# Retention visits with the crossed half of the values issued ahead of the next chunk's scores

## The chip, the cores and the metric

One Trainium2 chip, one core of it. The time is the device time of one execution in microseconds (us). Kernels that are compared ran in turns on the same chip. "TensorE" is the matrix engine (PE in the profile, PEld its weight loads), "VectorE" is DVE, "ScalarE" is ACT.

## The reference, cut to what matters

```python
# retention: 4 batches, 8 heads, 768 steps, head width 64
for t in range(S):
    state = gamma * state + k[t] (outer) v[t]
    y[t]  = scale * q[t] @ state
# then x = y as (3072, 512), and an MLP
h = x @ w_in                                   # 512 -> 2048
g = h * erf(softplus(h))
out = g @ w_out                                # 2048 -> 512
```

The kernel computes retention in 24 chunks of 128 steps. After the first 512 tokens it interleaves one chunk, a "visit", with each half-group of the MLP: visits j = 7 to 23 are the ones that the change touches. All arithmetic is fp32.

## The kernel before: the parts that matter

A visit works on 64-row, 64-column tiles of the array, so that four small matmuls are in it at once. A chunk is two half chunks of 64 steps. The scores inside a half are masked (`AM`) and applied to the values; the "straight" half of these products (`of_values(False)`) goes into the r banks of PSUM, the "crossed" half (`of_values(True)`) must go elsewhere. It goes into `other`, the two hp banks that also take the scores of the next chunk: scores in columns 0 to 63 of each head pair, crossed values in columns 64 to 127.

```python
def sub_scores(j):                                          # L485 is its matmul: 16 of 64x64
    for hp in range(HP):
        for a, s in itertools.product(range(2), range(2)):
            ...
            nc.tensor.matmul(SC[j][s][t, hp, :D], KT[j][own, hp, t], QT[j][own, hp, t], start=True, stop=True)

def sub_mask(j):                                            # L492: two VectorE operations
    AM[j] = ret.tile([P, 2, HP, C], F32, name="am")
    for s in range(2):
        nc.vector.tensor_tensor(AM[j][:, s, :, :D], SC[j][s][:, :, :D], causal_d[...], op=ALU.mult)

def sub_visit(j, g):
    ...
    other = SC[j + 1] = [ret_psum(ps_h) for _ in range(2)]  # the two hp banks

    def of_values(crossed):                                 # L535: 8 of 64x64
        ...
        nc.tensor.matmul(other[a][own, u % 2, D:] if crossed else pp[a][own, u % 2, t],
                         V[j][t, 2 * u + r, :], AM[j][t, r, u, :D], ...)

    if c:
        of_state(0)                                         # L520: 8 of 64x64
    ...                                                     # L556: products that renew the state
    nc.vector.tensor_tensor(state, state, new[0], op=ALU.add)   # L561 (a copy, L563, where c == 0)
    of_values(False)
    if j + 1 < NJ:
        sub_scores(j + 1)
        sub_mask(j + 1)
    of_values(True)
    of_state(1)                                             # L520 again, with the renewed state
    ...                                                     # ScalarE copies and VectorE adds to xT
```

Cuts are marked with dots. Counts of matmuls in the comments and in the text are calls of `nc.tensor.matmul`. The trace shows each of these calls as two MATMULs and two weight loads, so x16 in a line of the profile is 8 calls. After a visit TensorE goes on with the projection of the MLP (L784) on the full array.

## Time and profile before

| | before |
|---|---|
| time, median of 4 runs | 712.20 us (711.41 to 713.44) |
| span of the profiled execution | 711.2 us |
| TensorE busy | 688.0 us, 97% |
| VectorE, ScalarE busy | 54%, 36% |
| one visit, first load of the straight values to first load of the projection | 2.41 us |
| from one visit to the next | 27.9 us |

The busy line says which engine is the bound. The waits say where it stands still, the chain of waits says whether that standing still sets the end, and the timeline of a single visit gives the lengths. A word on the third row: a matmul that has started counts as busy until its modelled end, so a wait that begins while one is in flight is partly booked as busy time. The prediction below shows the lines.

### The profile page before, as it was taken

The numbers are of one execution on the slowest core, as the hardware profiler recorded it, in microseconds if no ns is written. First come the engines' busy times: TensorE is split into PE (matmuls) and PEld (weight loads), VectorE is DVE, ScalarE is ACT, GpSimd is POOL, SyncE is SP. The second block draws the span as 40 slices with busy tenths as digits, with TensorE's granted clock in tenths as the row PEclk, the third lists the DMA queues.
The fourth block names the chain that finished last, engine by engine and source line by source line (L and its number), as shares of the span: only waits on it lengthen the run. The fifth ranks groups of instructions, "written<-read, shape, count | busy, mean of one in ns | idle before, by whom it ended". The sixth has DMA issues, their size and how long they took to land.

```text
span 711.2 us, 14317 instructions
## 1 busy us (share of the span) xinstructions
PE 688.0 (97%) x6214; PEld 583.6 (82%) x6214; DVE 385.3 (54%) x581; ACT 256.9 (36%) x291; POOL 6.6 (1%) x21
## 2 busy tenths in 40 slices
PE   8798999999999999999999999999999999999997
PEld 7544454486998998998988989989989889899996
DVE  4689999264954553553554454544553463253234
ACT  3256462325144144143242341441432423414431
POOL 1000000010000000000000000000000000000000
PEclk9999999999999999999999999999999999999999
DMA  9999863102322221222222222312221210000000
GB/s 189 205 252 240 196 180 75 28 1 42 103 37 39 72 42 34 70 36 44 61 44 42 66 40 42 70 36 42 46 60 31 44 47 1 2 30 1 2 30 30
DMA packets 147215, 47.11 MB, mean 66 GB/s; under 512 B 135760, under 2 KB 136016, under 8 KB 147152
## 3 DMA queue, kind: packets, MB, share of 16 engines
q1 hardware_dynamic: 144640, 45.66, 29.4%
q10 hardware_dynamic: 2512, 0.53, 0.5%
q8 instruction: 48, 0.79, 0.5%
q14 instruction: 15, 0.12, 0.1%
HBM read 39.86 MB, written 6.29 MB: 65 GB/s over the span
## 4 chain that ended last, share of the span: by engine, by line
PE 90%; DVE 4%; DMA 3%; SPq 1%; issue 1%; ACT 0%; DVEq 0%
PE hp L712 35%; PE o L784 34%; PE o L655 8%; PE hp L642 4%; PE hp L535 2%; DMA w_in_sb<-in_moe_w_in_dram 2%; PE r L520 1%; PE hp L485 1%; DVE am L492 1%; PE o L556 1%; DMA w_out_sb<-in_moe_w_out_dram 1%; SPq L114 1%; DVE w_out_sb L211 1%; DMA kq<-in_q_dram 1%; PE r L535 1%
## 5 line engine op out<-in xcount | busy, mean ns | idle before, releaser
L712 PE MATMUL hp<-xs,w_in_sb 128*128 128x128 f32 x1280 | 149.8, 275 | 0.0
L712 PEld LDWEIGHTS hp<-xs,w_in_sb 128*128 128x128 f32 x1280 | 147.8, 192 | 1.6 <-issue 0.5
L784 PE MATMUL o<-w_out_sb,h 128*128 128x256 f32 x640 | 141.7, 379 | 0.0
L784 PEld LDWEIGHTS o<-w_out_sb,h 128*128 128x128 f32 x640 | 121.6, 190 | 16.5
L712 PE MATMUL hp<-xT,w_in_sb 128*128 128x128 f32 x960 | 113.7, 275 | 0.0
L712 PEld LDWEIGHTS hp<-xT,w_in_sb 128*128 128x128 f32 x960 | 111.9, 192 | 1.9 <-issue 1.0
L784 PE MATMUL o<-w_out_sb,e 128*128 128x256 f32 x480 | 112.1, 383 | 0.0
L631 DVE TENSOR_TENSOR e<-h,e 128x1024 f32<-128x1024 f32 x42 | 49.5, 1221 | 102.7 <-ACT e L612 102.7
L784 PEld LDWEIGHTS o<-w_out_sb,e 128*128 128x128 f32 x480 | 88.2, 190 | 11.6
L642 PE MATMUL hp<-xT,w_in_sb 128*128 128x512 f32 x128 | 56.5, 595 | 1.3 <-ACT h L645 0.9
L737 DVE TENSOR_TENSOR h<-h,hp 128x512 f32<-128x512 f32 x20 | 13.7, 686 | 75.3 <-PE hp L712 75.3
L607 ACT ACT_TABLE_LOAD x24 | 30.8, 1283 | 60.9 <-issue 45.5
L642 PEld LDWEIGHTS hp<-xT,w_in_sb 128*128 128x128 f32 x128 | 23.9, 190 | 30.2 <-issue 28.2
L612 ACT ACTIVATE e<-e 128x2048 f32<-128x2048 f32 (+1 forms) x23 | 42.2, 1837 | 0.2
L607 ACT ACTIVATE e<-h 128x2048 f32<-128x2048 f32 x22 | 42.0, 1910 | 0.2
L725 DVE TENSOR_TENSOR h<-h,hp 128x512 f32<-128x512 f32 x20 | 13.8, 689 | 51.4 <-PE hp L712 51.4
L574 ACT COPY xT<-r 128x256 f32<-128x256 f32 x32 | 10.4, 375 | 71.9 <-PE r L520 71.9
L735 ACT COPY h<-hp 128x512 f32<-128x512 f32 x20 | 11.7, 586 | 60.2 <-PE hp L712 60.2
L730 ACT COPY h<-hp 128x512 f32<-128x512 f32 x20 | 11.7, 587 | 57.9 <-PE hp L712 57.9
L728 ACT COPY h<-hp 128x512 f32<-128x512 f32 x20 | 11.7, 587 | 55.3 <-PE hp L712 55.3
L612 ACT ACT_TABLE_LOAD x24 | 30.8, 1283 | 0.4
L723 ACT COPY h<-hp 128x512 f32<-128x512 f32 x20 | 11.8, 588 | 48.6 <-PE hp L712 48.6
(123 smaller groups left out, 685.2 us busy)
## 6 DMA issues: line engine op xcount, KB each, us to landing
w_out_sb<-in_moe_w_out_dram SPq DMA_DIRECT2D x14, 512.0 KB, 5.6
kq<-in_k_dram SPq DMA_DIRECT2D x24, 256.0 KB, 3.5
v<-in_v_dram SPq DMA_DIRECT2D x24, 256.0 KB, 3.1
w_in_sb<-in_moe_w_in_dram SPq DMA_DIRECT2D x12, 512.0 KB, 9.1
out_dram<-r SPq DMA_DIRECT2D x23, 256.0 KB, 2.4
kq<-in_q_dram SPq DMA_DIRECT2D x256, 16.0 KB, 1.7
kb<-in_k_dram SPq DMA_DIRECT2D x256, 16.0 KB, 1.7
w_out_sb<-in_moe_w_in_dram SPq DMA_DIRECT2D x4, 512.0 KB, 7.8
```

The source lines that it names most:

```text
L535: nc.tensor.matmul(other[a][own, u % 2, D:] if crossed else pp[a][own, u % 2, t], V[j][t, 2 * u + r, :], AM[j][t, r, u, :D], start=crossed ...
L607: nc.scalar.activation(E[g], HS[g], AF.Softplus)
L612: nc.scalar.activation(E[g][:, half], E[g][:, half], AF.Erf)
L631: nc.vector.tensor_tensor(E[g][:, half], HS[g][:, half], E[g][:, half], op=ALU.mult)
L642: nc.tensor.matmul(p, w_in_of(ft, kk), XC[0][:, kk, :], start=(kk == 0), stop=(kk == n_k - 1))
L655: nc.tensor.matmul(O[0][tt].rearrange("p (d c) -> p d c", d=2), E[g][:, u * TCH + tt * P : u * TCH + (tt + 1) * P], w_out_of(ft), start=(f ...
L712: nc.tensor.matmul(bank[:, u, :], w_in_sb[:, s, IN[a], kk, u * P : (u + 1) * P], XS[m][b][:, kk, :], start=(p in (1, 2, 5) and u == 0 and ...
L723: nc.scalar.copy(h["11"], flat)
L725: nc.vector.tensor_tensor(h["11"], h["11"], flat, op=ALU.add)
L728: nc.scalar.copy(h["12"], flat)
L737: nc.vector.tensor_tensor(h["12"], h["12"], flat, op=ALU.add)
L784: nc.tensor.matmul(O[m][i][:, half, :], G[g][a][:, u * P : (u + 1) * P], w_out_sb[:, s, OUT[b], u, :], start=i not in started, stop=(s == ...
```

## The change

Its intent: take the masks' read of the hp banks out from between two writes of TensorE to these banks.

```diff
         of_values(False)
+        of_values(True)
         if j + 1 < NJ:
             sub_scores(j + 1)
             sub_mask(j + 1)
-        of_values(True)
         of_state(1)
```

## The prediction

> **What bounds the kernel now.** I read the page's busy line first, then the waits of TensorE and of its weight loads, then the chain of work that ended last, and at the end the timeline of single visits of retention.
>
> The page, busy time by engine (us, share of the span, instructions):
>
> ```profile
> PE 688.0 (97%) x6214; PEld 583.6 (82%) x6214; DVE 385.3 (54%) x581; ACT 256.9 (36%) x291; POOL 6.6 (1%) x21
> ```
>
> TensorE is the bound: 97% busy, and in the whole-kernel chain it holds 90% of the span. VectorE and ScalarE have half of their time and more free. So a gap of TensorE is time, and an instruction of another engine is time only where TensorE waits for it.
>
> The waits (who waited for whom: us in total, times, longest):
>
> ```profile
> PE hp L535 <- DVE am L492: 8.5, 16, 0.5
> PEld hp L535 <- DVE am L492: 10.7, 16, 0.7
> ```
>
> These are the longest waits of TensorE and of its weight loads for another engine; all the others of TensorE are from the first part of the kernel. L535 are the matmuls of the values, those that go to the hp banks are the crossed half; L492 is the mask on the next chunk's scores. 16 waits, one for each visit that has a next chunk to score: the visits are j = 7 to 23, and the last has none.
>
> The chain through one visit (start us, us, what; "x16" counts matmuls and weight loads together, so 8 matmuls):
>
> ```profile
> 383.79 0.23 PE r L535 x16
> 384.03 0.54 PE hp L485 x32
> 384.56 0.42 DVE am L492
> 384.98 0.04 issue
> 385.02 0.32 PE hp L535 x2
> 385.35 0.01 issue
> 385.36 0.40 PE hp L535 x11
> 385.75 0.01 PE r L520
> 385.76 0.05 PE hp L535 x3
> 385.81 0.23 PE r L520 x15
> 386.04 0.41 PE o L784
> ```
>
> The mask is on the chain. And it costs more than the wait that the table above counts: the first crossed matmul starts when the first of the two masks is done (385.02), the second waits for the second mask (385.36), and only then do the other six stream. The table's 8.5 us leaves that second wait out, because one matmul is in flight in it.
>
> The timeline of the same visit (start us, us, engine, line; idle before in brackets):
>
> ```profile
> 383.56 0.33 PEld L535 LDWEIGHTS r<-am,v 64*64 64x64 f32 x16
> 383.79 0.56 PEld L485 LDWEIGHTS hp<-qT,kT 64*64 64x64 f32 x32
> 383.85 0.42 DVE L561 TENSOR_TENSOR state<-state,o 128x256 f32<-128x256 f32 x1 [0.18 <-PE r L556]
> ...
> 384.55 0.76 DVE L492 TENSOR_TENSOR am<-hp,causal_d 128x256 f32<-128x256 f32 x2 [0.28 <-PE hp L485]
> 385.02 0.59 PEld L535 LDWEIGHTS hp<-am,v 64*64 64x64 f32 x13 [0.67 <-DVE am L492]
> ...
> 385.97 1.59 PEld L784 LDWEIGHTS o<-w_out_sb,e 128*128 128x128 f32 x8
> ```
>
> From the first weight load of the first half of the values (383.56) to the first one of the projection that follows (385.97) a visit takes 2.41 us. This is the stretch that the change rearranges. I read it from the starts of weight loads, as the ends of matmuls are modelled.
>
> **What the Trainium skill says.** "PSUM — Partial Sum Buffer", section "PSUM bank collisions raise a hardware error": two engines may not touch one bank in the same quadrant of partitions at once, even in different columns, so an access is to be guarded by the bank and not by the address. The trace of before agrees in its effect: the mask reads columns 0 to 63 of each head pair, the crossed values write columns 64 to 127, no datum passes between them, and TensorE waited all 16 times. It is a wait made by sharing, and an order of issue can take it away.
>
> "TensorEngine Tiling (Array Packing)", section "Key Properties": tiles of the array run independently, but a change of the tiling mode drains the array. The trace agrees with the first: sixteen 64x64 matmuls of L556, modelled at 0.22 us each, go from 383.09 to 383.56, 0.47 us, so 29 ns each. For the second see the last visit below. All matmuls that are exchanged are 64x64, so no mode change is added.
>
> "TensorE: Matmul & The Clock Gate", section "Wait — 56ns, not 53.3ns?": however small a matmul, starts are about 25 ns or more apart. The 29 ns above lie a little over that, so I expect no small matmul to go faster than 29 ns after the change.
>
> **The change part by part.** It removes no instruction and adds none; VectorE's, ScalarE's and the DMA queue's orders are the same. On TensorE, in each of the 16 visits, eight crossed values pass ahead of sixteen scores. The order of writing in the two hp banks becomes crossed values, scores, then the masks read; after that nothing of TensorE touches these banks in the visit.
>
> - Removed: the wait of the crossed values for both masks. The compiled order shows what they wait for instead: for the previous reader of the hp banks (ScalarE for the first, VectorE's addition L737 for the second). The scores waited for just that before, at the same place of the stream, so this moves and doesn't grow. In most visits it is satisfied in time (L737 from 382.97 for 0.69 us, so 383.66, against 383.79); in four visits before, the scores' loads show some 0.05 to 0.15 us of it, and they will keep it.
> - Added: the second product with the state, L520, gets a wait of its own for the state's addition L561, which the wait for the masks used to cover. L561 ends at 384.27.
> - New length of the stretch: 8 values 0.235, 8 crossed 0.235, 16 scores 0.47 (all at 29 ns), then the 8 products with the state and the change to the projection's full array. The last visit, which has no scores, shows that tail already:
>
> ```profile
> 634.46 0.13 PEld L535 LDWEIGHTS r<-am,v 64*64 64x64 f32 x1
> ...
> 635.26 0.32 PEld L520 LDWEIGHTS r<-qT,state 64*64 64x64 f32 x16 [0.19 <-DVE state L561]
> ...
> 635.65 1.38 PEld L784 LDWEIGHTS o<-w_out_sb,e 128*128 128x128 f32 x7
> ```
>
> From L520's first load to L784's first is 0.39 us: 0.235 of issue and some 0.155 of drain. The sum is 0.235 + 0.235 + 0.47 + 0.39 = 1.33 us, against 2.41: 1.08 us less in a visit. The chain gives the same in another way: 386.04 - 383.79 = 2.25 us before, and 40 matmuls at 29 ns are 1.17 us after, also 1.08 less. The visits that are longer before (2.47 to 2.54 us) are so by the wait for L737, which stays, so the gain is taken to be equal. 16 x 1.08 = 17.3 us, all of it on TensorE's own path. 712.74 - 17.3 = 695.4; I allow 0.2 us for small bubbles: **695.6 us**, 2.4% less.
>
> **The rivals.**
>
> First, a wait for the state takes the place of the mask's. In the last visit L520 waits 0.19 us for L561 with nothing but the crossed values before it. With sixteen scores between, L520 is due at 383.56 + 0.235 + 0.235 + 0.47 = 384.50, and the state is ready at 384.27 plus the 0.05 us that a release took there (L535 at 385.02 after a mask that ended by 384.97). 0.18 us of slack, and against it that TensorE may need its release some time ahead of the moment of use. If it all went wrong by 0.2 us a visit, 3.2 us are lost: 698.8.
>
> Second, the gain is only what the waits' table says, 16 x 0.53 = 8.5 us on TensorE or 10.7 on its weight loads, because the second half of the wait is hidden anyway. That would give 702 to 704. Against it: at 385.36 the chain itself shows six crossed matmuls and eight products still to come, whose time lies behind both masks.
>
> Third, what TensorE gains it gives back at a later wait, as the gating or the transposes have less time. For this: the gate's exponentials share one buffer. Against it: the elements of a group are gated by VectorE at 370.7, and the projection that needs them comes at 377.5, 7 us later; ScalarE's wait before the copies of retention's result is 4.3 us; the mask itself is needed a whole visit later, 28 us. A visit shorter by 1 us can't use up 7. VectorE's mask will start some 0.23 us later, beside ScalarE's copies from other banks, and TensorE waits for neither. I give this little weight. A lower granted clock, now 0.997, with a busier array has as little for it.
>
> **Range and chances.** The gain in a visit could lie between 0.9 (a bubble at L520 or slower streaming of 40 mixed matmuls) and 1.18 us (the drain shorter): 14.4 to 18.9 us, so 693.8 to 698.3. I take 693.8 to 699.0 as the range, with the longer side at the slow end. The 2% line lies at 698.5, a gain of 0.89 us in a visit. The first rival in full would just miss it, the second and third would miss it clearly: together 0.13. Slower would need a new wait longer than the one removed: 0.01 at most. So faster 0.86, same 0.13, slower 0.01.
>
> **What would show each step.** In the waits of TensorE, the line L535 on L492 must be gone, and no line of 16 waits of more than 0.1 us each take its place; a line L520 on L561 would be the first rival. In a visit's timeline, the stretch from the first load of the first values to the projection's first load must be near 1.33 us and the distance between two visits shrink from 27.9 to 26.8 us. TensorE's busy share should rise to 98 or 99% with the instructions' counts unchanged. If the stretch shrinks by 1.08 us but the distance between visits less, the third rival holds; if the stretch shrinks by about 0.5, the second.

## The result, and the profile after

The changed kernel took 695.06 us in the median of 4 runs (694.28 to 696.97) against 712.20 us before. The ratio is 0.9762, with a 95% interval of 0.9735 to 0.9789. Ratios here are the mean time of one kernel's fast runs over that of the other's of the same rounds, so not quite the ratio of the medians. The results are correct.

The busy line of the page after:

```profile
PE 679.8 (98%) x6214; PEld 579.7 (84%) x6214; DVE 383.8 (55%) x581; ACT 257.2 (37%) x291; POOL 6.6 (1%) x21
```

The instructions are the same in number. The span fell by 711.2 - 694.0 = 17.2 us, and TensorE's busy time fell by 688.0 - 679.8 = 8.2 us of that, although it does the same matmuls: those 8.2 us were waiting that had been booked as busy. The other 9.0 us were booked as idle. So the idle column of before showed only about half of what there was to gain.

The longest waits of TensorE after, and below the dots the one line of its weight loads on the state (us in total, times, longest):

```profile
PE r L461 <- DVE am L433: 2.7, 2, 2.5
PE r L408 <- issue: 1.6, 2, 1.0
...
PEld r L520 <- DVE state L561: 0.2, 1, 0.2
```

The line of 16 waits of L535 on L492 is gone; what leads now is from the first part of the kernel, and it was there before. The single wait on the state is that of the last visit, also there before.

The chain of waits through the same visit as in the prediction, j = 14 (start us, us, what):

```profile
374.99 0.23 PE r L535 x16
375.23 0.23 PE hp L535 x16
375.46 0.47 PE hp L485 x32
375.93 0.23 PE r L520 x16
376.16 0.41 PE o L784
```

No other engine is in it any more: 376.16 - 374.99 = 1.17 us, against 386.04 - 383.79 = 2.25 before.

The timeline of this visit after (start us, us, engine, line; idle before in brackets):

```profile
374.76 0.33 PEld L535 LDWEIGHTS r<-am,v 64*64 64x64 f32 x16
374.99 0.33 PEld L535 LDWEIGHTS hp<-am,v 64*64 64x64 f32 x16
375.23 0.56 PEld L485 LDWEIGHTS hp<-qT,kT 64*64 64x64 f32 x32
375.69 0.33 PEld L520 LDWEIGHTS r<-qT,state 64*64 64x64 f32 x16
375.98 0.76 DVE L492 TENSOR_TENSOR am<-hp,causal_d 128x256 f32<-128x256 f32 x2 [0.51 <-PE hp L485]
376.09 1.16 PEld L784 LDWEIGHTS o<-w_out_sb,e 128*128 128x128 f32 x6
```

From 374.76 to 376.09 the stretch is 1.33 us instead of 2.41. The masks now run to 376.74, well into the projection, and nothing of TensorE stands behind them. The next visit's first load is at 401.57, 26.81 us later, where before two such visits lay 27.89 us apart (383.56 to 411.45): the 1.08 us is kept all the way to the next visit.

The stretch in the kinds of visit, read in the same way from the timelines:

| visits | before, us | after, us | less |
|---|---|---|---|
| 11 of j = 8 to 22 | 2.41 or 2.42 | 1.33 or 1.34 | 1.08 |
| j = 7 | 2.51 | 1.44 | 1.07 |
| j = 11, 17 (end of a batch) | 2.47 | 1.38 | 1.09 |
| j = 12, 18 (start of a batch) | 2.54 | 1.47, 1.48 | 1.07, 1.06 |
| j = 23 (no next scores) | 1.19 | 1.19 | 0 |

Without the last row these are 39.08 us before and 21.79 after, 17.3 less: the whole gain in time.

### The profile page after: what moved, and what is told of

Read it like the earlier page. It is cut to its first block, busy times and chain, and to the rows that moved or that the text cites. A ratio compares the mean times of both kernels' runs of the same rounds, so it can differ in the third digit from the quotient of the medians.

```text
span 694.0 us, 14331 instructions
## 1 busy us (share of the span) xinstructions
PE 679.8 (98%) x6214; PEld 579.7 (84%) x6214; DVE 383.8 (55%) x581; ACT 257.2 (37%) x291; POOL 6.6 (1%) x21
## 4 chain that ended last, share of the span: by engine, by line
PE 91%; DVE 3%; DMA 2%; SPq 1%; issue 1%; ACT 0%; POOL 0%; DVEq 0%; POOLq 0%
PE hp L712 36%; PE o L784 35%; PE o L655 8%; PE hp L642 4%; DMA w_in_sb<-in_moe_w_in_dram 2%; PE r L520 1%; PE hp L485 1%; PE o L367 1%; PE o L556 1%; SPq L114 1%; DMA w_out_sb<-in_moe_w_out_dram 1%; DVE w_out_sb L211 1%; PE hp L535 1%; PE r L408 1%; PE r L535 1%
```

## The experiments

The theory: the masks' read stands between two writes of TensorE to the same banks, so the end of both masks is on TensorE's path, 1.08 us in each of 16 visits. The rivals: the new order of the small matmuls streams better as such; only the first mask's wait of 0.53 us counts; the product with the state is about to take the wait's place; the wait moved to a later place. In kernels with added lines the line numbers behind the addition shift by one or two.

**The changed kernel again**, on the chip of the next three runs.

> The changed kernel once more, beside its relatives on one chip. Theory (the crossed values stood behind the masks only because they share banks with the scores; 1.08 us in each of 16 visits): ratio to the kernel before 0.976. A difference of chips or of the day instead: a ratio away from 0.976 by more than 0.003.

694.84 us against 712.03, ratio 0.9760 (0.9747 to 0.9774), and the same stretches as above. The result repeats.

**The masks issued later, the order of TensorE left as it was before.**

```diff
         of_values(False)
         if j + 1 < NJ:
             sub_scores(j + 1)
-            sub_mask(j + 1)
         of_values(True)
+        if j + 1 < NJ:
+            sub_mask(j + 1)
         of_state(1)
```

> The order of TensorE stays that of the kernel before (scores, then crossed values); only the two masks are issued after the crossed values instead of between. Theory: what cost the time is the masks' read standing between two writes to a bank, not the order of scores and values, so the whole gain appears: stretch of a visit 1.33 us instead of 2.41, ratio 0.976. Rival (the order of the small matmuls on the array is what matters, values and scores stream better in the new order): no gain or a small part of it, ratio 0.99 to 1.00, stretch over 2 us.

695.04 us, ratio 0.9761 (0.9748 to 0.9774), the same as the changed kernel within its noise. One visit of it:

```profile
374.63 0.33 PEld L535 LDWEIGHTS r<-am,v 64*64 64x64 f32 x16
374.86 0.56 PEld L485 LDWEIGHTS hp<-qT,kT 64*64 64x64 f32 x32
375.33 0.33 PEld L535 LDWEIGHTS hp<-am,v 64*64 64x64 f32 x16
...
375.85 0.76 DVE L492 TENSOR_TENSOR am<-hp,causal_d 128x256 f32<-128x256 f32 x2 [0.51 <-PE hp L535]
375.96 1.16 PEld L785 LDWEIGHTS o<-w_out_sb,e 128*128 128x128 f32 x6
```

Here the scores still come ahead of the crossed values, and the stretch is 1.33 us too. So the order of scores and values is of no account: what cost the time was the read between them. The brackets show the other side of the sharing: now VectorE's masks wait for the crossed values, with which they share no datum, and that costs nothing. The first rival falls.

**The wait filled with other work.** In the kernel before, the second product with the state goes into the gap.

```diff
             sub_mask(j + 1)
-        of_values(True)
         of_state(1)
+        of_values(True)
```

> The kernel before, with the second product with the state moved ahead of the crossed values, so that eight matmuls fill the wait for the masks. Theory: the masks' end is what the crossed values stand on, so only the time of those eight (8 x 29 ns, 0.235 us) is hidden: stretch 2.17 us, the gain 16 x 0.235 = 3.8 us, ratio 0.9947. Rival (only the first mask's wait counts, the wait of 0.53 us in the table, and it is partly hidden anyhow): the same or less. Rival (any other work in the gap takes most of the gap away): ratio below 0.985.

708.35 us, ratio 0.9949 (0.9937 to 0.9962); the stretch is 2.18 us. Filling the gap hides what is put into it, eight matmuls, and no more; to remove the wait is worth 4.6 times as much (17.2 us against 3.7). One visit:

```profile
381.43 0.32 PEld L520 LDWEIGHTS r<-qT,state 64*64 64x64 f32 x16
381.66 0.76 DVE L492 TENSOR_TENSOR am<-hp,causal_d 128x256 f32<-128x256 f32 x2 [0.28 <-PE hp L485]
...
382.14 0.65 PEld L535 LDWEIGHTS hp<-am,v 64*64 64x64 f32 x16 [0.38 <-DVE am L492]
382.85 1.16 PEld L784 LDWEIGHTS o<-w_out_sb,e 128*128 128x128 f32 x6
```

The eight crossed loads last from 382.14 to 382.79, 0.65 us, where the undisturbed ones above last 0.33: that is the wait for the second mask, which no idle column shows. This is against the rival that only the first wait counts.

**The masks doubled, in both kernels.** Each mask is computed twice, with the same result.

```diff
-        for s in range(2):
+        for s in (0, 0, 1, 1):
             nc.vector.tensor_tensor(AM[j][:, s, :, :D], ...
```

In the kernel before:

> The kernel before, with each of the two masks computed twice (same values written again). Theory: both masks' time is on TensorE's path, so the second crossed matmul waits for two more masks; masks follow one another by 0.34 us, so the stretch grows by 0.67 us to 3.1 us and the time by 16 x 0.67 = 10.8 us, ratio 1.015. Rival (only the first mask's wait counts, or the wait is hidden by something else that ends at the same time): half of that or nothing, ratio 1.000 to 1.008.

735.69 us, ratio 1.0340 (1.0323 to 1.0357): 24 us more, over twice what I expected, so this expectation missed. Two things came together. The chain of a visit shows the first:

```profile
393.52 0.42 DVE am L492
393.94 0.02 issue
393.96 0.77 DVE am L492 x2
394.73 0.02 issue
394.75 0.43 DVE am L492
395.18 0.04 issue
```

A repeated mask writes what the one before it wrote and waits for its end, so a repetition costs 0.44 us and not the 0.34 by which two different masks follow each other. The stretch became 3.33 us, 0.92 more, and 16 x 0.92 = 14.7 us. The second is the clock. Five of the distances between visits are not 28.8 but 30.3 to 30.6 us. The stretches around the start of one of them (us, busy of each engine, then PEclk, the granted clock, DMA share, GB/s):

```profile
275.50:277.50 2.00, 1.12 (x33) 0.92 (x34) 1.11 (x3) 0.07 (x1) 0.00 (x0) 1.00 0.60 130
277.50:281.50 4.00, 4.00 (x12) 3.21 (x13) 3.67 (x8) 0.58 (x2) 0.00 (x0) 0.57 0.24 38
281.50:285.50 4.00, 4.00 (x20) 3.54 (x19) 0.25 (x1) 2.69 (x2) 0.00 (x0) 1.00 0.21 34
```

After this visit the granted clock fell to 0.57 in the mean of 4 us and came back. Read more finely, each of the five falls is to 0.50 for 3.41 us. They begin at 277.7, 308.4, 482.5, 513.2 and 544.0 us, whole multiples of 3.413 us apart, and in the 3.41 us before each one TensorE was busy for only 1.95 to 1.97 us. A fall costs 1.6 to 1.7 us, the five together about 8 us; with 14.7 it accounts for 23 of the 24. In the kernel before and in the changed one no 2 us of the middle part is below 0.95, so this is of the experiment's making and no part of the gain.

In the changed kernel:

> The changed kernel, with each of the two masks computed twice. Theory: nothing of TensorE waits for a mask inside the visit, the next reader comes a whole visit later, so VectorE's extra 0.67 us a visit costs nothing: ratio to the kernel before 0.976, stretch 1.33 us. Rival (the wait was moved to a later reader, with little room left): ratio 0.98 or more, and a wait for the masks or for VectorE's later additions turns up on TensorE.

694.84 us, ratio 0.9762 (0.9747 to 0.9777), stretch 1.33 us, no new wait on TensorE. The same work of VectorE that cost 24 us in the order of before costs nothing here. The mask is off the path, and the clock didn't fall, so VectorE's extra work by itself isn't what lowers it. The rival of a wait moved to a later place falls with it.

**Two runs to settle the miss.** Only the second mask doubled, in the kernel before (`for s in (0, 1, 1)`):

> The kernel before, with only the second mask computed twice; a repeated mask has been seen to follow its first by 0.44 us. Theory (the masks' end is on TensorE's path one for one, and what went beyond it with both masks doubled was the granted clock, which fell to half for some 3.4 us after 5 of 16 visits): stretch 2.41 + 0.44 = 2.85 us, 16 x 0.44 = 7.0 us, ratio 1.010, with the clock at 1.00 in the middle of the kernel. Rival (a doubled mask costs more than its time for another reason): ratio over 1.015 with the clock at 1.00.

719.87 us, ratio 1.0109 (1.0092 to 1.0126); stretch 2.87 us, the clock at 1.00 from 160 us to the end. One repetition of 0.44 us gives 0.46 us in the stretch and 16 x 0.46 = 7.4 us: the end of the masks is on the path one for one. Both masks doubled and the wait filled with the product with the state (the last two diffs together):

> Both masks doubled, as in the run that took 735.7 us, but with the second product with the state moved into the wait, so that TensorE is idle 0.235 us less in each visit. By the path alone: stretch 3.33 - 0.235 = 3.10 us, 16 x 0.69 = 11.0 us over the kernel before, ratio 1.0155. If the granted clock falls by TensorE's idle share of a few microseconds, fewer than 5 visits are followed by the low clock, and the ratio is 1.016 to 1.025; if it falls for another reason (VectorE's work), about 5 again and 1.027.

722.86 us, ratio 1.0150 (1.0134 to 1.0165); stretch 3.10 us, and in the profiled execution not one visit is followed by a low clock. It differs from the run of 735.7 us by eight matmuls that moved into the gap: TensorE's counted idle time in a visit is 0.70 + 0.46 = 1.16 us, and was 0.99 + 0.46 = 1.45 us there. This agrees with a clock that falls by the idle time of TensorE, but it doesn't show it: it is one pair of kernels, and the two ran on different chips. The traces add this. If the span of the run of 735.7 us is cut into pieces of 3.413 us that end where the falls begin, eleven of them have TensorE busy for only 1.95 to 1.97 us, and five of the eleven are followed by a fall. In the run here, cut in the same way from its own change of the clock at the end, the lowest piece has 2.20 us. Where in a visit a piece begins would thus be part of why not every visit was hit; why six equally low pieces were not followed by a fall, these runs don't tell.

**How near the state's wait is.** In the changed kernel, the scores moved to the end:

```diff
         of_values(True)
+        of_state(1)
         if j + 1 < NJ:
             sub_scores(j + 1)
             sub_mask(j + 1)
-        of_state(1)
```

> The changed kernel, with the scores and the masks moved behind the second product with the state. Nothing waits for the masks here either. Theory with the first rival of the prediction in it: the state's addition is ready some 0.76 to 0.80 us after the first load of the values, the product is now due at 0.47 us and waits 0.33 us, as it does in the last visit of both kernels; stretch 1.66 us, 16 x 0.33 = 5.3 us more than the changed kernel, ratio 0.9835, and a line of 17 waits of L520 on L561. Rival (the state has much more room than I worked out): ratio 0.976 and no such waits.

698.66 us, ratio 0.9815 (0.9801 to 0.9828). The wait is there, in 14 visits in the table of waits, and shorter in the other three:

```profile
377.39 0.32 PEld L520 LDWEIGHTS r<-qT,state 64*64 64x64 f32 x16 [0.20 <-DVE state L561]
```

It is smaller than I expected. The state's addition ends 0.71 us after the first load of the values, and L520 starts at 0.76; I had taken 0.80, from the last visit, where the addition runs later (to 0.74 or 0.75). The stretch is 1.62 us, 0.29 more instead of 0.33. In the visits that wait for the banks anyway (j = 7, 12, 18) it is only 0.15 to 0.18 more, as the two waits overlap. Over all visits the stretches of the profiled execution are 4.2 us longer, and the medians of the time differ by 3.8 us, instead of 5.3.

Then, in the changed kernel in its own order, copies of 128x128 on VectorE ahead of the state's addition, one or three:

```diff
+        for _ in range(3):                   # and range(1)
+            nc.vector.tensor_copy(causal, causal)
         if c:
             nc.vector.tensor_tensor(state, state, new[0], op=ALU.add)
```

> The changed kernel, with one copy of 128x128 on VectorE ahead of the state's addition. VectorE is idle for 0.18 us there, the copy takes some 0.2 us, so the addition ends a few hundredths of a us later; the slack of the product with the state is 0.14 to 0.18 us. Theory: no change, ratio 0.976, L520 waits in no visit but the last. Rival (there is no slack, the release is needed well ahead of its use): a small wait in every visit, ratio 0.977 to 0.979.

695.68 us, ratio 0.9772 (0.9758 to 0.9787). The time alone can't tell the two expectations apart, as the interval holds both. The trace can: in the ordinary visits the copy runs from 0.02 to 0.24 us after the first load, in VectorE's idle time, the addition keeps its place, the stretch is 1.33 us and L520 waits in the last visit alone. It is a weak test, for the addition was hardly moved: in three visits only, by 0.06 us (j = 7) and 0.1 us (j = 12, 18), without a wait.

> The changed kernel, with three copies of 128x128 on VectorE ahead of the state's addition in the 15 visits that add. The addition then ends some 0.41 us later (three copies of 0.2 us less the 0.18 us of idle time), which is 0.24 us past the slack. Theory: L520 waits for L561 by some 0.24 us in each of these visits, the stretch grows from 1.33 to 1.57 us, 15 x 0.24 = 3.6 us, ratio 0.981. Rival (the slack is larger than I read): ratio 0.976.

698.57 us, ratio 0.9813 (0.9798 to 0.9828), stretch 1.53 or 1.54 us in the ordinary visits:

```profile
404.40 0.41 DVE L563 TENSOR_TENSOR state<-state,o 128x256 f32<-128x256 f32 x1
...
404.86 0.32 PEld L520 LDWEIGHTS r<-qT,state 64*64 64x64 f32 x16
405.25 0.73 PEld L786 LDWEIGHTS o<-w_out_sb,e 128*128 128x128 f32 x4
```

The values' first load is at 403.72, so the addition ends 1.09 us later instead of 0.71, and L520 starts at 1.14, where it was due at 0.93. A delay of 0.38 us costs 0.21 us: the slack is 0.17 us. (The copies ran in all 17 visits, not in the 15 of my expectation.)

**Left open.** A version in which the crossed values have banks of their own, with nothing else changed, could not be made: all eight banks are in use, and the one free half of an r bank is written by the other half of the array's rows at that time. That it is the shared bank is therefore shown by taking the read away from between the writes, not by taking the sharing away. No run pointed to a version that beats the changed one; what is left in a visit beyond the 40 matmuls is 0.15 us at the change to the full array, in three visits (j = 7, 12, 18) 0.10 to 0.14 us of waiting for the previous readers of the hp banks, and in two (j = 11, 17) 0.05 us at the first values.

## Why the prediction was right, point by point

- **TensorE is the bound, and a gap of it is time.** Right: 17.3 us less in the stretches of the visits, 17.2 us less in the span.
- **The wait costs more than the table of waits says.** Right. The table had 8.5 us; 8.2 us more were booked as busy, and the filled gap shows the second mask's wait inside "busy" loads.
- **40 matmuls at 29 ns and a tail of 0.39 us, 1.33 us in all.** Right to 0.01 us. The chain after has 0.23, 0.23, 0.47 and 0.23 us for the four parts. One reading behind it was wrong: a line's x16 doesn't count matmuls and weight loads together, it counts 16 MATMULs, two for a call. So 29 ns is the mean for a call and not the distance between two starts: in the visit shown after, four MATMULs start within 0.02 us, and the next four 0.06 us after the first four. The sums go by calls and hold.
- **The wait for the previous readers of the hp banks moves and doesn't grow.** Right where there is such a wait, but the visits were not all read rightly. Those that wait are j = 7, 12 and 18, with 0.10 to 0.14 us before and after. In j = 11 and 17 the extra 0.05 us is no wait for these banks: there only eight products of L556 come before the values, on two of the four tiles, and the first values start beside the last of them, 0.05 us ahead of the next ones. The gain in these visits is the same 1.09 us, so the sum is not touched.
- **First rival, the state's wait.** It doesn't happen, for the reason given: L520 was expected at 0.94 us with 0.18 us of slack, it starts at 0.93, and the delayed addition measured 0.17. Of the worry that a release is needed ahead of its use nothing is seen: L520 starts 0.05 us after the addition's end where it does wait.
- **Second rival, half the gain.** Wrong, as argued: the gain per visit is 1.08 us, not 0.53.
- **Third rival, the gain given back.** Wrong: the visits moved together by 1.08 us (27.89 to 26.81), and doubled masks cost nothing after the change.
- **The size.** 695.6 us predicted, 695.06 measured. The prediction started from 712.74 us, the median of the three runs known then; against 712.20, the median of four, the fall is 17.1 us, as predicted. Single runs spread over 2 to 3 us, so whether the 0.2 us set aside for bubbles were needed can't be told.

What was not foreseen is outside of the prediction: that in an experiment with a wait only 0.9 us longer the clock would fall.

## What to carry to other kernels

Where two pieces of work share a PSUM bank only to save space, look at the order of the accesses of the engines to the bank. Here all writes first and then the read by the other engine cost TensorE nothing, as the banks were needed again only much later; the read between two writes cost it 1.08 us in each visit, and every lengthening of that read came on top one for one. Size such a wait from the starts of the instructions around it, or from the chain, not from the idle column: with small matmuls about half of it was booked as busy. And before moving work up, find the next wait that the old one covered, and its slack; here it was 0.17 us, and the neighbouring order with the scores last gave 3.8 of 17 us back.

## What the Trainium skill lacked or had wrong

- "TensorE: Matmul & The Clock Gate", section "HAM oscillation — how this bites in real kernels", gives as the rule no idle gap of TensorE above about 3.4 us. With both masks doubled no counted gap of TensorE in the visits was longer than 0.99 us, 1.45 us in all in a visit, and the granted clock fell to 0.50 for 3.41 us after 5 of 16 visits. So a gap of 3.4 us is not needed. The page itself tells, in "A second HAM failure mode: psum-queue depth-cycling", of a clock that swings with frequent short idling, but gives no length for it. With 1.16 us in a visit, in one run on another chip, it did not fall.
- "TensorEngine Tiling (Array Packing)", section "Key Properties", says that a change of the tiling mode drains the array, without a cost. Here eight 64x64 matmuls take 0.39 us to the first load of the full array, where eight matmuls followed by others of their kind take 0.235: some 0.155 us more at the change. No run varied the tiling alone, so that the drain is the cause is not shown.
- "PSUM — Partial Sum Buffer", section "PSUM bank collisions raise a hardware error", says to guard by the bank, but not what such a guard can cost: a read of two banks between two runs of writes took 1.08 us of TensorE's path, and the same read behind both took none.
